# Four buffers for float32 queries and keys, fill products through the first tile, and POOL in place of ACT for one step of the weight conversion

## The chip, the cores and the metric

The kernel runs on one core of a Trainium2 chip. The metric is the device time of one execution in microseconds, as the median of several runs. Five engines work side by side, each through its own list of instructions in a fixed order: PE (matrix products), ACT and DVE (elementwise work), POOL, and SP, which here only starts transfers. "PEld" is the loading of the stationary operand of a product.

## The reference, cut to what matters

Attention over 4 batches of 8 heads, with 512 local and 32 global positions, is followed by two dense blocks on 2304 tokens of width 512:

```python
out = concat([softmax(q_g k_all^T) v_all, softmax(mask(q_l k_l^T), q_l k_g^T) v_all])   # window of +-32
h = x @ w_in                                  # 512 -> 2048
x = g(h) @ w_out                              # g: 0 below -1, h above 1, (h + 1)^2 / 4 between
y = ((x @ w_a) * (x @ w_b)) @ w_out2          # 512 -> 1536 -> 512
```

The weights arrive as float64.

## The kernel before, in words

The tokens go through in six tiles of up to three blocks of 128. One attention item is one block and one pair of heads; a tile has 12 items (the last one differs). `att_atoms` runs items as a pipeline: scores `s` of item k (L187, two products), softmax (L200 on DVE, L204 on ACT, L208 to L211), transposes `tp` of item k-2 (L217), their copy on ACT (L221), values `o` of item k-3 (L227), and a copy to `xraw` (L231). Items of the first nine blocks hold q and k in float32 (`qk`, loaded at L158 into a tag with 2 buffers, up to 3 items ahead, L342); later ones hold split halves (`qkd`, `qs`, `kh`, `kl`). The first four items are each followed by two products of the identity matrix with itself that nobody reads (`warm`, L192, `NWARM` and `WARM_ITEMS`).

Tile 0's attention runs first, alone, with a step of the weight stream at every eighth piece of it. Then `x_split` makes float32r halves of its result (L402 on ACT, L403 on DVE) and the first dense block begins: `h_unit` (12 products into `hp`, L435 to L437 in the helper `mm3`) and `x_unit` (12 products into `acc`). The stages are: 6 units of tile 0 beside tile 1's attention, 16 units of tile 1, the other 10 units of tile 0, then tiles 2 to 5, each beside the attention of a later tile, and last the second dense block. Tile 0 is written to memory and read back in between (L416, L422).

A weight slice comes as 512 KB of float64 (`wraw`, L90) and is rebuilt as float32 in `w_conv`: the high word is scaled on ACT into `wt` (L98), then DVE shifts it (L99) and puts in sign and low bits (L100, L101); `split` then makes halves on ACT (L108) and DVE (L109). There are 68 such conversions: 32 of the first block's weights, of which 4 fall in tile 0's attention and the others in the next two stages, 24 of w_a and w_b after that, and 12 of the last weights. `wraw` has 2 buffers, `wt` 3. In the second stage a conversion is put behind the rectifier work of the unit before (`paced`).

The order on each engine comes from a scheduler that fills in from the code's order and from what each instruction waits for, so a small edit shifts rows far away.

Of the kernel before, what the change touches and what calls it, by code (L numbers as in the profile page):

```python
# [10 lines left out]
F32 = mybir.dt.float32  # L11
# [3 lines left out]
AF = mybir.ActivationFunctionType  # L15
# [4 lines left out]
P = 128  # L20
# [7 lines left out]
KW = SG + P + 2 * WIN  # L28
KC = KW // 2
# [9 lines left out]
W_DOWN = 2.0 ** -111  # L39
# [5 lines left out]


NNAT = 9
NWARM, WARM_ITEMS = 2, 4
FA = 6
START_ATOMS = 8  # L50
LEAD1 = 4
# [8 lines left out]
def body(tc, qk, qkd, vw, kg, vg, w1i, w1o, w2a, w2b, w2o, mask, out):  # L60
    nc = tc.nc
# [4 lines left out]
    ps = es.enter_context(tc.tile_pool(name="ps", bufs=4, space=PSUM))  # L66
# [4 lines left out]
    ident = cp.tile([P, P], F32, name="ident")  # L71
# [6 lines left out]
    def f32(t):  # L78
        return t.bitcast(F32)
# [13 lines left out]
    def w_conv():  # L93
        key, raw = wq.pop(0)
        low, high = raw[:, :, 0], raw[:, :, 1]
        t = sp["p"].tile([P, 512], I32, name="wt", bufs=sp["wt"])
        tf = f32(t)
        nc.scalar.activation(tf, f32(high), AF.Copy, scale=W_DOWN)  # L98
        nc.vector.tensor_scalar(t, t, 3, 0x7FFFFFFF, ALU.logical_shift_left, ALU.bitwise_and)  # L99
        nc.vector.scalar_tensor_tensor(t, high, -0x80000000, t, ALU.bitwise_and, ALU.bitwise_or)  # L100
        nc.vector.scalar_tensor_tensor(t, low, 29, t, ALU.logical_shift_right, ALU.bitwise_or)  # L101
        return key, tf
# [8 lines left out]
    def w_split():  # L111
        key, tf = w_conv()
        w = slot()
        split(w[:, 0], w[:, 1], tf)
        wslots[key] = w
# [23 lines left out]
    def new_xraw(t):  # L139
        xraw_cur[t] = [mp.tile([P, 384], F32, name=f"xraw{c}", bufs=1) for c in range(NC)]  # L140

    gp = {}

    class Local:
        def __init__(self, t, j, blk, p):
# [6 lines left out]
        def load(self):  # L152
            if self.stk:
                self.raw = gp["k"].tile([P, 2, P + KW], F32, name="qkd", tag="qkd", bufs=2)
                nc.sync.dma_start(self.raw, qkd[self.blk - NNAT, self.p])
            else:
                self.qk = gp["k"].tile([P, P + KW], F32, name="qk", tag="qkd", bufs=2)
                nc.sync.dma_start(self.qk, qk[self.blk, self.p])  # L158

        def prep(self):  # L160
# [28 lines left out]
        def fill(self):  # L189
            w = ps.tile([P, 512], F32, name="warm", tag="acc")  # L190
            for _ in range(NWARM):
                nc.tensor.matmul(w[:, :P], ident, ident, start=True, stop=True)  # L192

        def s_post(self):
            m = 1 if self.i == 0 else (2 if self.i == SL // P - 1 else 0)
            self.e = ap.tile([P, 2, KW], F32, name="e", tag="e", bufs=EBUFS)
            mn = ap.tile([P, 2], F32, name="mn", tag="mn", bufs=EBUFS)
            self.sm = ap.tile([P, 2], F32, name="sm", tag="sm", bufs=EBUFS)
            for h in range(2):
                nc.vector.tensor_tensor_reduce(  # L200
                    self.e[:, h], self.s[h], masks[:, m], -SCALE, 3.0e38,
                    ALU.add, ALU.min, mn[:, h:h + 1])
            for h in range(2):
                nc.scalar.activation(self.e[:, h], self.e[:, h], AF.Exp, bias=mn[:, h:h + 1],  # L204
                                     scale=-1.0, accum_out=self.sm[:, h:h + 1])
# [17 lines left out]
        def v_pe(self):  # L223
            self.o = ps.tile([P, P], F32, name="o", tag=self.tag)
            for c in range(2):
                for h in range(2):
                    nc.tensor.matmul(self.o[64 * h:64 * h + 64], self.v[:, c, 64 * h:64 * h + 64],  # L227
                                     self.pt[:KC, 2 * c + h], start=c == 0, stop=c == 1)

        def v_post(self):  # L230
            nc.vector.tensor_copy(xraw_cur[self.t][self.p][:, self.j * P:(self.j + 1) * P], self.o)  # L231
# [92 lines left out]
    items = []  # L324
    ends = {}
# [11 lines left out]
    def att_atoms():  # L337
        n = len(items)
        nl = nv = npr = 0
        started = set()  # L340
        for k in range(n + 3):
            while nl < min(k + (2 if nl < n and isinstance(items[nl], Glob) else 3), n):  # L342
                items[nl].load()
                nl += 1
            while npr < min(k + 1, nl):
                items[npr].prep()
                npr += 1
            while nv < min(k, n):
                items[nv].load_v()
                nv += 1  # L350
            if k < n and items[k].t is not None:
                it = items[k]
                it.s_pe()
                if k < WARM_ITEMS:
                    it.fill()
                it.s_post()
            if 1 <= k <= n and items[k - 1].t is not None:
                items[k - 1].norm()
            while npr < min(k + 2, nl):
                items[npr].prep()  # L360
                npr += 1
            if k < n and items[k].t is not None:
                yield k, 0
            if 2 <= k <= n + 1 and items[k - 2].t is not None:
                it = items[k - 2]
                it.t_pe()
                it.t_post()
                yield k, 1
            if 3 <= k and items[k - 3].t is not None:
                it = items[k - 3]  # L370
                if isinstance(it, Local) and it.t not in started:
                    started.add(it.t)
                    new_xraw(it.t)
                it.v_pe()
                it.v_post()
                yield k - 3, 2

    att = att_atoms()
    done = {"n": 0}

# [80 lines left out]
    acc = {}  # L461
# [112 lines left out]
    def w2_conv():  # L574
        r = w_conv()
        rawn[0] += 1
        raw_to(rawn[0] + sp["raw"])
        return r
# [108 lines left out]
    k = 0  # L687
# [83 lines left out]
    for u in range(len(units)):  # L771
        for kind in (0, 1):
            if kind == 0:
# [17 lines left out]
                if u in conv_at:  # L791
                    i = conv_at.index(u)
                    (nm, f2), tf = paced(w_conv)
                    nc.sync.dma_start(wd[f2]["ab".index(nm)], tf)
                    if i + 2 < len(ab2):
                        w_load(*ab2[i + 2])
# [152 lines left out]
```

## Time and profile before

| | us |
|---|---|
| median of 3 runs | 948.53 (947.63 to 950.57) |
| the profiled execution, its own time | 954.25 |
| its span, first to last instruction | 952.5 |
| busy: PE / DVE / ACT / POOL | 932.2 / 717.1 / 530.1 / 0.7 |
| first product of the first dense block | 49.97 from the start |
| tile 0's products begin again after the read back | 184.55 |

Busy times count an engine as busy while one of its instructions is under way. Products overlap, so PE's busy share says little about how dense they are; the step from one group of products to the next says more. The granted clock of PE is given as a share of full speed: 1.00 is 2.4 GHz, 0.50 is 1.2 GHz.

### The profile page before, as it was taken

The numbers are of one execution on the slowest core, as the hardware profiler recorded it, in microseconds if no ns is written. First come the engines' busy times: TensorE is split into PE (matmuls) and PEld (weight loads), VectorE is DVE, ScalarE is ACT, GpSimd is POOL, SyncE is SP. The second block draws the span as 40 slices with busy tenths as digits, with TensorE's granted clock in tenths as the row PEclk, the third lists the DMA queues.
The fourth block names the chain that finished last, engine by engine and source line by source line (L and its number), as shares of the span: only waits on it lengthen the run. The fifth ranks groups of instructions, "written<-read, shape, count | busy, mean of one in ns | idle before, by whom it ended". The sixth has DMA issues, their size and how long they took to land.

```text
span 952.5 us, 16671 instructions
## 1 busy us (share of the span) xinstructions
PE 932.2 (98%) x5964; PEld 840.9 (88%) x5964; DVE 717.1 (75%) x1863; ACT 530.1 (56%) x1271; POOL 0.7 (0%) x7
## 2 busy tenths in 40 slices
PE   6999999999999999999999999999999999999997
PEld 4577888899999999987889999999999999999996
DVE  5688999789877877764449968888896666877663
ACT  6677766566666766644445555555654444654441
POOL 0000000000000000000000000000000000000000
PEclk9699999999999999999999999999999999999999
DMA  5465555666534453323455323321241111131101
GB/s 174 151 214 164 177 161 168 219 223 211 178 117 156 128 162 112 120 94 103 133 194 183 96 77 115 95 68 51 69 147 45 45 45 49 42 121 56 56 12 56
DMA packets 59299, 114.05 MB, mean 120 GB/s; under 512 B 7248, under 2 KB 28368, under 8 KB 59216
## 3 DMA queue, kind: packets, MB, share of 16 engines
q1 hardware_dynamic: 59072, 112.81, 37.8%
q8 instruction: 47, 0.77, 0.3%
q14 instruction: 36, 0.29, 0.1%
q10 hardware_dynamic: 144, 0.17, 0.1%
HBM read 95.40 MB, written 17.56 MB: 119 GB/s over the span
## 4 chain that ended last, share of the span: by engine, by line
PE 90%; DMA 4%; DVE 3%; ACT 1%; issue 1%; SPq 0%; ACTq 0%; DVEq 0%
PE hp L435 7%; PE acc L435 6%; PE acc L436 6%; PE hp L437 6%; PE hp L436 6%; PE acc L437 6%; PE pb L596 5%; PE pb L597 5%; PE pb L594 5%; PE py L661 5%; PE py L662 5%; PE py L660 5%; PE px L594 4%; PE px L597 4%; PE px L596 4%; PE o L227 4%
## 5 line engine op out<-in xcount | busy, mean ns | idle before, releaser
L435 PE MATMUL hp<-xh,w 128*128 128x384 f32 (+1 forms) x384 | 130.7, 341 | 3.4 <-ACT xh L402 1.7
L435 PE MATMUL acc<-g,w 128*128 128x384 f32 (+1 forms) x384 | 131.1, 341 | 0.0
L436 PE MATMUL acc<-g,w 128*128 128x384 f32 (+1 forms) x384 | 127.0, 331 | 0.0
L437 PE MATMUL acc<-g,w 128*128 128x384 f32 (+1 forms) x384 | 125.6, 329 | 0.0
L437 PE MATMUL hp<-xl,w 128*128 128x384 f32 (+1 forms) x384 | 125.2, 327 | 0.0
L436 PE MATMUL hp<-xh,w 128*128 128x384 f32 (+1 forms) x384 | 125.1, 326 | 0.0
L108 ACT ACTIVATE w<-wt 128x512 fp32r<-128x512 f32 (+1 forms) x116 | 65.2, 563 | 72.6 <-PE pb L597 44.9
L596 PE MATMUL pb<-w 128*128 128x384 f32 (+1 forms) x288 | 94.7, 329 | 0.0
L597 PE MATMUL pb<-w 128*128 128x384 f32 (+1 forms) x288 | 94.3, 327 | 0.0
L594 PE MATMUL pb<-w 128*128 128x384 f32 (+1 forms) x288 | 93.8, 326 | 0.0
L723 ACT ACTIVATE r<-hp,half 128x384 f32<-128x384 f32 (+1 forms) x96 | 53.4, 557 | 55.1 <-PE hp L437 54.3
L435 PEld LDWEIGHTS hp<-xh,w 128*128 128x128 f32 x384 | 72.4, 189 | 10.8 <-issue 3.1
L724 DVE SCALAR_TENSOR_TENSOR m<-hp,r 128x384 f32<-128x384 f32 (+1 forms) x96 | 51.0, 532 | 39.9 <-ACT r L723 39.5
L661 PE MATMUL py<-w,g 128*128 128x512 f32 x204 | 80.7, 396 | 0.0
L662 PE MATMUL py<-w,g 128*128 128x512 f32 x204 | 80.7, 396 | 0.0
L660 PE MATMUL py<-w,g 128*128 128x512 f32 x204 | 79.7, 390 | 0.0
L435 PEld LDWEIGHTS acc<-g,w 128*128 128x128 f32 x384 | 72.4, 189 | 6.9 <-issue 5.3
L109 DVE TENSOR_TENSOR w<-wsum,w 128x256 fp32r<-128x256 f32 (+1 forms) x108 | 54.6, 507 | 29.8 <-ACT w L108 29.8
L728 ACT ACTIVATE g<-m 128x384 fp32r<-128x384 f32 (+1 forms) x96 | 48.3, 503 | 47.9 <-DVE m L725 47.4
L436 PEld LDWEIGHTS acc<-g,w 128*128 128x128 f32 x384 | 72.5, 189 | 2.1 <-issue 1.4
L437 PEld LDWEIGHTS acc<-g,w 128*128 128x128 f32 x384 | 72.2, 188 | 1.2 <-issue 1.0
L109 DVE TENSOR_TENSOR w<-wt,w 128x512 fp32r<-128x512 f32 (+1 forms) x116 | 70.2, 605 | 3.5 <-ACT w L108 1.7
(113 smaller groups left out, 2119.6 us busy)
## 6 DMA issues: line engine op xcount, KB each, us to landing
wt<-wd SPq DMA_DIRECT2D x72, 256.0 KB, 2.7
qkd<-in_qkd_dram SPq DMA_DIRECT2D x28, 352.0 KB, 3.1
wraw<-in_w1i_dram SPq DMA_DIRECT2D x16, 512.0 KB, 3.6
wraw<-in_w1o_dram SPq DMA_DIRECT2D x16, 512.0 KB, 3.4
v<-in_vw_dram SPq DMA_DIRECT2D x64, 112.0 KB, 2.4
qk<-in_qk_dram SPq DMA_DIRECT2D x36, 176.0 KB, 2.7
wraw<-in_w2a_dram SPq DMA_DIRECT2D x12, 512.0 KB, 3.9
wraw<-in_w2b_dram SPq DMA_DIRECT2D x12, 512.0 KB, 4.2
```

The lines of the kernel that those rows point to most:

```text
L108: nc.scalar.activation(hi, src, AF.Copy)
L109: nc.vector.tensor_tensor(lo, src, f32(hi), ALU.subtract)
L435: nc.tensor.matmul(acc, whi, xhi, start=first, stop=False)
L436: nc.tensor.matmul(acc, wlo, xhi, start=False, stop=False)
L437: nc.tensor.matmul(acc, whi, xlo, start=False, stop=last)
L594: nc.tensor.matmul(out[:, :n], w[:, 0, r], hi[:, c, :n], start=start and c == 0, stop=False, skip_group_check=True)
L596: nc.tensor.matmul(out[:, :n], w[:, 1, r], hi[:, c, :n], start=False, stop=False, skip_group_check=True)
L597: nc.tensor.matmul(out[:, :n], w[:, 0, r], lo[:, c, :n], start=False, stop=k in (1, 5, 6) and c == 1, skip_group_check=True)
L660: nc.tensor.matmul(a, gh[:, c], w[:, 0], start=f == 0, stop=False)
L661: nc.tensor.matmul(a, gh[:, c], w[:, 1], start=False, stop=False)
L662: nc.tensor.matmul(a, gl[:, c], w[:, 0], start=False, stop=f == NF2 - 1)
L723: at["act"] = nc.scalar.activation(r[:, :W], hp[:, :W], AF.Relu, bias=half, scale=0.5 / W_UP).ins
```

## The change

There are three edits. First, float32 `qk` tiles rotate over four buffers: two of the old tag and one each in the tags of `kh` and `kl`, which the later items use; the load may now run up to five items ahead instead of three. Second, `warm` follows each of the 12 items of tile 0 instead of four, and a new `bridge` of 8 such products is placed behind the last value product of tile 0. Third, the scaling of the high word in `w_conv` is a `tensor_scalar_mul` on POOL instead of an ACT instruction, for all 68 conversions.

```diff
-NWARM, WARM_ITEMS = 2, 4
+NWARM, WARM_ITEMS = 2, 12
+NBRIDGE = 8
...
-        nc.scalar.activation(tf, f32(high), AF.Copy, scale=W_DOWN)
+        nc.gpsimd.tensor_scalar_mul(tf, f32(high), W_DOWN)
...
-                self.qk = gp["k"].tile([P, P + KW], F32, name="qk", tag="qkd", bufs=2)
+                n = nat["n"] % 4
+                nat["n"] += 1
+                if n < 2:
+                    self.qk = gp["k"].tile([P, P + KW], F32, name="qk", tag="qkd", bufs=2)
+                else:
+                    self.qk = gp["k"].tile([P, P + KW], F32, name="qk", tag=("kh", "kl")[n - 2], bufs=1)
...
+        def bridge(self):
+
+            with tc.issue_after(self.oi):
+                w = ps.tile([P, 512], F32, name="bridge", tag="acc")
+                for _ in range(NBRIDGE):
+                    nc.tensor.matmul(w[:, :P], ident, ident, start=True, stop=True)
...
-            while nl < min(k + (2 if nl < n and isinstance(items[nl], Glob) else 3), n):
+            while nl < n and nl < k + (2 if isinstance(items[nl], Glob) else 3 if items[nl].stk else 5):
...
+                if k - 3 == ends[0] - 1:
+                    it.bridge()
```

In the rows of the changed program the lines are those of its own file: scores are L194 (before L187), `warm` L199 (L192), transposes L231 (L217), values L241 (L227), `mm3` L452 to L454 (L435 to L437), the exponential L218 (L204), the copies L224 and L235 (L210 and L221), the scaling L99 (L98) and the shift L100 (L99).

SP's first transfers, before:

```order
1 L158 DMA qk<-in_qk_dram 128x352 x2
2 L90 DMA wraw<-in_w1i_dram 128x1024 x2
3 L158 DMA qk<-in_qk_dram 128x352 x2
4 L174 DMA v<-in_vw_dram 112x256 x3
5 L158 DMA qk<-in_qk_dram 128x352 x2
```

and SP's first transfers now:

```order
1 L165 DMA qk<-in_qk_dram 128x352 x4
2 L91 DMA wraw<-in_w1i_dram 128x1024
3 L165 DMA qk<-in_qk_dram 128x352
4 L91 DMA wraw<-in_w1i_dram 128x1024
5 L165 DMA qk<-in_qk_dram 128x352
```

The third and fourth `qk` stand ahead of both weight slices, and the second slice stands behind a fifth `qk` that reuses a buffer.

PE's first rows, before (`s` are scores, two rows to an item):

```order
7 L187 MATMUL s_208<-qk 128x224
8 L192 MATMUL warm<-ident 128x128 x6
9 L217 MATMUL tp<-ident,e 112x128 x4
10 L187 MATMUL s_209<-qk 128x224
11 L192 MATMUL warm<-ident 128x128 x2
12 L217 MATMUL tp<-ident,e 112x128 x4
13 L227 MATMUL o<-pt,v 64x128 x4
```

and the same place on PE now:

```order
9 L194 MATMUL s_251<-qk 128x224
10 L194 MATMUL s_252<-qk 128x224
11 L199 MATMUL warm<-ident 128x128 x6
12 L231 MATMUL tp<-ident,e 112x128 x4
13 L199 MATMUL warm<-ident 128x128 x2
14 L231 MATMUL tp<-ident,e 112x128 x4
15 L241 MATMUL o<-pt,v 64x128 x4
16 L199 MATMUL warm<-ident 128x128 x2
17 L231 MATMUL tp<-ident,e 112x128 x4
18 L241 MATMUL o<-pt,v 64x128 x4
```

Before, three and a half items' scores stood ahead of the first fill; now five items' scores do, and a fill of two goes on with every item.

PE where tile 0's attention ends, before (`hp` is the first dense product):

```order
53 L227 MATMUL o<-pt,v 64x128 x4
54 L187 MATMUL s_607<-qk 128x224
55 L187 MATMUL s_608<-qk 128x224
56 L217 MATMUL tp<-ident,e 112x128 x4
57 L227 MATMUL o<-pt,v 64x128 x4
58 L435 MATMUL hp<-xh_635,w 128x384
59 L436 MATMUL hp<-xh_635,w 128x384
```

and PE at that place now:

```order
63 L241 MATMUL o<-pt,v 64x128 x4
64 L231 MATMUL tp<-ident,e 112x128 x4
65 L452 MATMUL hp<-xh_672,w 128x384
66 L241 MATMUL o<-pt,v 64x128 x4
67 L206 MATMUL bridge<-ident 128x128 x8
68 L453 MATMUL hp<-xh_672,w 128x384
69 L454 MATMUL hp<-xl_677,w 128x384
```

The first dense product moved ahead of the last value product, and the bridge stands between it and the others.

ACT's first rows, before:

```order
3 L204 ACTIVATE e,sm<-e,mn 128x224 x4
4 L210 ACTIVATE e<-e,sm 128x224
5 L98 ACTIVATE wt<-wraw 128x512
6 L204 ACTIVATE e,sm<-e,mn 128x224 x2
7 L210 ACTIVATE e<-e,sm 128x224
8 L204 ACTIVATE e,sm<-e,mn 128x224
9 L98 ACTIVATE wt<-wraw 128x512
```

and ACT's first rows now:

```order
3 L218 ACTIVATE e,sm<-e,mn 128x224 x4
4 L224 ACTIVATE e<-e,sm 128x224
5 L218 ACTIVATE e,sm<-e,mn 128x224 x2
6 L224 ACTIVATE e<-e,sm 128x224
7 L218 ACTIVATE e,sm<-e,mn 128x224 x2
8 L235 ACTIVATE pt<-tp 112x512
9 L224 ACTIVATE e<-e,sm 128x224
```

The scaling rows left ACT; they are 68 rows on POOL now, and DVE's shift waits for POOL where it waited for ACT.

## Rows read from the trace of the kernel before

**Rows 1.** Busy time of each engine in stretches of the span, PE's granted clock.

```profile
core 0: us, PE busy (x) PEld busy (x) DVE busy (x) ACT busy (x) POOL busy (x), PEclk, DMA share, GB/s
...
15.00:25.00 10.00, 9.28 (x78) 5.91 (x78) 8.68 (x40) 9.06 (x27) 0.00 (x0) 1.00 0.64 210
28.90:45.60 16.70, 16.32 (x73) 9.78 (x72) 9.35 (x43) 10.38 (x33) 0.00 (x0) 0.50 0.50 151
50.00:185.00 135.00, 132.32 (x829) 112.08 (x830) 124.63 (x349) 95.58 (x230) 0.00 (x0) 1.00 0.56 178
185.00:900.00 715.00, 713.85 (x4641) 661.21 (x4641) 536.12 (x1322) 383.83 (x906) 0.00 (x0) 1.00 0.36 112
900.00:952.50 52.50, 47.48 (x273) 42.87 (x271) 27.19 (x59) 17.27 (x39) 0.00 (x0) 0.98 0.11 36
```

**Rows 2.** Chain that ended last, up to 50 us: start, duration, what.

```profile
5.07 3.69 DMA qk<-in_qk_dram
...
8.90 1.83 PE s L187 x6
10.73 2.86 PE warm L192 x12
13.59 0.85 PE tp L217 x4
...
15.36 0.64 PE warm L192 x4
...
22.18 4.86 DMA qk<-in_qk_dram
...
27.80 2.40 DMA qk<-in_qk_dram
```

**Rows 3.** Timeline of PE up to 50 us: start, duration, group, idle time ahead.

```profile
16.36 0.66 PE L227 MATMUL o<-pt,v 112*64 112x128 f32 x8
16.95 0.65 PE L187 MATMUL s<-qk 64*128 64x224 f32 x4
17.53 0.65 PE L217 MATMUL tp<-ident,e 128*112 128x128 f32 x4
18.11 0.66 PE L227 MATMUL o<-pt,v 112*64 112x128 f32 x8
...
24.78 0.66 PE L227 MATMUL o<-pt,v 112*64 112x128 f32 x8
27.08 0.65 PE L187 MATMUL s<-qk 64*128 64x224 f32 x4 [1.65 <-DMA qk<-in_qk_dram]
...
47.66 0.66 PE L227 MATMUL o<-pt,v 112*64 112x128 f32 x8
49.97 0.44 PE L435 MATMUL hp<-xh,w 128*128 128x384 f32 x1 [1.65 <-ACT xh L402]
```

**Rows 4.** Chain, later in the half-clock stretch: start, duration, what.

```profile
33.50 1.04 PE s L187 x2
34.54 1.03 PE tp L217 x4
35.57 1.05 PE o L227 x8
```

**Rows 5.** The step that moves, over the whole span: busy, mean ns, idle ahead of it.

```profile
L98 ACT ACTIVATE wt<-wraw 128x512 f32<-128x512 f32 x68 | 45.1, 665 | 17.0 <-DVE w L109 7.3 <-DMA wraw<-in_w1o_dram 3.7 <-DMA wraw<-in_w1i_dram 3.2
```

**Rows 6.** All groups of POOL above 128x1, and one of 128x1: busy, mean ns.

```profile
masks.py:199 POOL TENSOR_SCALAR_AFFINE_SELECT ident<-ident 128x128 f32<-128x128 f32 x1 | 0.3, 293 | 0.0
masks.py:197 POOL MEMSET ident<- 128x128 f32 x1 | 0.2, 204 | 0.3 <-POOLq L938 0.3
L74 POOL MEMSET half<- 128x1 f32 x1 | 0.1, 98 | 0.0
```

**Rows 7.** Groups of DVE between 50 and 185 us: busy, mean ns.

```profile
L100 DVE SCALAR_TENSOR_TENSOR wt<-wraw,wt 128x512 int32<-128x512 int32 x29 | 19.9, 687 | 0.1
L109 DVE TENSOR_TENSOR w<-wt,w 128x512 fp32r<-128x512 f32 x28 | 19.3, 689 | 2.1 <-ACT w L108 1.7
```

More of the change, by code (lines that the diff above doesn't have):

```diff
@@ L142, in body @@
     gp = {}
+    nat = {"n": 0}
     class Local:
@@ L226, in v_pe @@
                 for h in range(2):
-                    nc.tensor.matmul(self.o[64 * h:64 * h + 64], self.v[:, c, 64 * h:64 * h + 64],
-                                     self.pt[:KC, 2 * c + h], start=c == 0, stop=c == 1)
+                    self.oi = nc.tensor.matmul(
+                        self.o[64 * h:64 * h + 64], self.v[:, c, 64 * h:64 * h + 64],
+                        self.pt[:KC, 2 * c + h], start=c == 0, stop=c == 1).ins
         def v_post(self):
```

## The prediction

> **What bounds the kernel now.** I first read the busy times by stretch [rows 1]. From 185 to 900 us PE is busy 713.85 of 715 us at full clock, while DVE has 715 - 536 = 179 us to spare. There the products are the bound, so whatever moves the start of that stretch moves the end one for one. From 900 us the tail keeps its shape. What can change lies ahead of 185 us, in two parts.
>
> Tile 0's attention, to 49.97 us, is not bound by one engine. The chain of waits [rows 2] shows three causes. The first is loads of q and k: PE waits for them at 8.90 (issued at 5.07, when a buffer came free), at 27.08 (1.65 us idle [rows 3]) and around 28 to 30. The second is the clock: between 28.9 and 45.6 us it is granted at 0.50, that is 1.2 GHz, and each group of products steps by 1.04 us [rows 4] where it steps by 0.58 at full speed [rows 3]. It fell after PE had run dry waiting for a load, and rose after PE had run on without a break. The third is ACT, 9.06 of 10 us busy between 15 and 25 us [rows 1], while the clock was up.
>
> The stages from 50 to 185 us run both PE (132.3 of 135) and DVE (124.6 of 135) nearly full [rows 1]. DVE's spare time there is only 10 us, and 29 of the 68 conversions fall into it [rows 7].
>
> **The change part by part.** *Start of the pipeline.* Four `qk` now load at once, but in PE's new order the scores of the fifth item stand ahead of the first fill, and that item's load reuses a buffer, as the one did that was issued at 5.07 and took 3.69 us [rows 2]. So the fifth item's scores again start near 8.9. Before, six rows (1.83 us) followed there, now four (1.2 us); the fill of 2.86 us then begins near 10.1 instead of 10.73. The first transposes start near 13 instead of 13.59, and the first values (16.36 before [rows 3]), with one more fill ahead, near 15.4: 1 us gained.
>
> *Pace of the items.* From the first to the twelfth value group the trace needs 47.66 - 16.36 = 31.3 us, 2.85 us for each of 11 steps [rows 3]. At full clock four steps took 24.78 - 16.36 = 8.4 us, 2.10 each, of which PE's own work is 0.58 + 0.58 + 0.59 = 1.75 [rows 3]. A fill of two products adds 0.64 [rows 2], so PE needs 2.39 an item if it never stalls, and 2.10 + 0.64 = 2.74 if the fill adds to every stall. I take 2.5, nearer to the first: a fill runs mostly where PE would wait, and ACT, which held that stretch at 91%, loses 0.665 us with each of the four conversions [rows 1, 5]. This supposes that the clock stays up; PE then works 2.39 of 2.5 us, more densely than in any part of the stretch in which it was up before. The loads that broke the pace now have four buffers and are issued two items earlier. Eleven steps take 27.5 us instead of 31.3: 3.8 gained, with bounds of 26.3 (5.0 gained) and 30.1 (1.2 gained). The last two or three items have no fill, which gives up to 1.9 more at the lower end, and ACT and DVE have worked ahead by then; if PE never stalled at all, its groups from the first transposes on sum to 9 x 0.58 for scores, 9 x 0.64 for fills, 12 x 0.58 and 12 x 0.59 = 25 us, and the end would come 10 us earlier.
>
> *Bridge.* 8 products are 16 records, four fills of 0.64 = 2.6 us. Before, PE idled 1.65 us at that place for ACT's split [rows 3], which the bridge covers. Some dense products could have run there instead, so I charge 0.5 us (0 to 1). The first part thus gains 1 + 3.8 - 0.5 = 4.3; with the ACT relief beyond the pace and the missing last fills I take **5 us**, between 2 and 10.
>
> *Scaling on POOL, its own price.* The trace has no such instruction on POOL. The nearest rows are a MEMSET and an AFFINE_SELECT of 128x128 at 204 and 293 ns, against 98 ns for 128x1 [rows 6]. Per further element that is 0.83 to 1.5 ns, so 512 elements take an estimated 0.52 to 0.87 us; ACT took 0.665 [rows 5]. One conversion's chain changes by -0.14 to +0.21 us. I take no change: POOL has nothing else to do and can start when the slice lands, where ACT had to come round to it. ACT also no longer stands still for slices: it waited 3.7 + 3.2 us on such transfers with rectifier work queued behind it [rows 5]. PE's whole idle time from 50 to 185 us is 2.7 us [rows 1], so this is worth 0 to 2.7; I take **1 us**. The queue behind the wait is now DVE's, whose shift waits for POOL; behind it stand the rectifier steps and the softmax of the next item. It waited for ACT in the same way before, so nothing is added unless POOL is slow.
>
> *Scaling on POOL, its price for DVE.* While POOL reads and writes the buffers, DVE may be slowed. No row shows the two at work together, so I bound it: between nothing, and DVE standing still for the whole of each POOL instruction. 29 instructions of 0.52 to 0.87 us are 15 to 25 us, less the 10 us DVE has to spare: 5 to 15 us. I take **2 us**, nearer to nothing, because DVE also has steps with one operand in these buffers, and its spare 10 us absorb the first part. The 35 conversions behind 185 us lie beside 179 us of spare DVE time and 331 us of spare ACT time [rows 1] and cost nothing; if that cover failed, 35 x 0.87 = 30 us would be at stake.
>
> *SP.* In the new order the two first slices of w_a and w_b stand ahead of tile 0's read back instead of between its parts. PE's wait there is part of the 2.7 us above; I change nothing for it, with 1 us either way.
>
> **Sum.** -5 - 1 + 2 = -4 us. The profiled execution took 954.25 us (span 952.5) and would take 950.25. The median of the runs, 948.53, is 5.7 lower than the profiled execution; the same 4 us give **944.5 us**.
>
> **The rivals.** *POOL holds DVE up (slower).* Place: 50 to 185 us, where DVE is 92% busy. In the trace the two-operand steps fill much of DVE there, 19.9 and 19.3 us for two of its groups alone [rows 7], and POOL's instruction comes exactly where DVE works through the conversion before. The price is the 5 to 15 us above, plus some 2 us in tile 0's attention, against the 6 gained: -6 + 7 = +1 to -6 + 17 = +11, that is 949.5 to 959.5. It decides from about 0.6 us of delay to each of the 29. For it: DVE's small reserve. Against it: nothing in the trace, since POOL does nothing in these stretches [rows 1].
>
> The Trainium skill names this mechanism (GPSIMD Engine Reference, section Key points): the engine shares its SBUF interfaces with VectorE, and contention arises with two-input instructions and two-port modes. No run here shows it yet. By that rule the time would lie in this rival's range and not at the sum's.
>
> *The clock falls all the same.* The fills cost 0.64 us at full clock and twice that at 0.50. If PE again runs dry and the last five items go at half speed, each takes 3.1 [rows 4] + 1.28 = 4.4 us instead of 2.5, 9.5 us more than forecast: 944.5 + 9.5 = 954. For it: the waits for ACT and DVE stay. Against it: the long waits for loads, after which it fell, go.
>
> *The gain is swallowed.* The fills add to every stall (2.74 an item), ACT's relief finds no taker, and DVE loses 3 to 4 us: about 947 to 950, no change that counts.
>
> *The items run as PE can.* Pace 2.39 and no cost on DVE: -9 to -12, that is 937 to 940.
>
> **How the numbers follow.** About 0.3% (2.8 us) is what a measurement of this kernel can tell from no change, so faster means below 945.7 and slower above 951.4. Forecast, 940 to 947: 0.47, three quarters of it below 945.7. Items at PE's pace: 0.19, all faster. Swallowed: 0.12, no change. POOL holds DVE up: 0.17, two thirds of it slower. Clock falls: 0.05, slower. That gives faster 0.35 + 0.19 = 0.54, no change 0.12 + 0.12 + 0.06 = 0.30, slower 0.11 + 0.05 = 0.16. The range leaves out the ends: 936.5 to 953.
>
> **What would show it.** In the profile after: the first dense product near 44 to 45 us instead of 49.97; the clock at 1.00 from 15 us on; the value groups 2.4 to 2.7 us apart; POOL's 68 instructions at 0.5 to 0.9 us; DVE's L100 and L109 (one line lower or so) still at 0.69 us between 45 and 180 us; tile 0's products back at 180 us instead of 184.55. I am wrong if those DVE groups grow by 0.2 us or more, if POOL's instruction takes over 1 us, or if the clock drops again before the first dense product.

## The result, and the profile after

The changed kernel takes 958.11 us (median of 10 runs, 956.25 to 959.47), the kernel before 953.97 us beside it: a ratio of 1.0064, with an interval of 1.0041 to 1.0088 (the quotient of the two medians is 1.0043; the kernel before varies much, 947.63 to 959.22 us in ten executions). It is slower by about 6 us, where the forecast was 944.5 us with a range up to 953. Of the 13.6 us between the forecast and the measured time, 5.4 lie in the kernel before, whose median was 948.53 us where the forecast started and 953.97 here; the rest is a change of +4 us instead of -4. The profiled execution of the changed kernel took 959.04 us, its span is 957.3 us.

Busy time of each engine by stretch, as in [rows 1], now of the changed kernel:

```profile
core 0: us, PE busy (x) PEld busy (x) DVE busy (x) ACT busy (x) POOL busy (x), PEclk, DMA share, GB/s
15.00:25.00 10.00, 10.00 (x85) 7.10 (x85) 9.37 (x39) 8.65 (x27) 3.20 (x2) 1.00 0.59 186
28.90:45.60 16.70, 15.99 (x131) 11.91 (x130) 15.88 (x62) 14.87 (x44) 4.66 (x3) 1.00 0.84 266
50.00:185.00 135.00, 127.17 (x779) 107.72 (x778) 118.34 (x320) 75.68 (x185) 44.50 (x27) 0.99 0.50 159
185.00:900.00 715.00, 711.85 (x4604) 655.11 (x4604) 535.91 (x1312) 360.26 (x864) 55.06 (x34) 1.00 0.35 110
900.00:957.30 57.30, 52.26 (x302) 47.44 (x300) 31.48 (x70) 19.44 (x44) 0.00 (x0) 0.98 0.12 37
```

The start did better than forecast. The clock is at 1.00 where [rows 1] show 0.50, and PE has no idle time between 15 and 25 us. The timeline of PE shows the first and the twelfth value group, the bridge, the dense products behind it, and far below the first product on tile 0's x that was read back:

```profile
14.16 0.66 PE L241 MATMUL o<-pt,v 112*64 112x128 f32 x8
...
38.85 0.66 PE L241 MATMUL o<-pt,v 112*64 112x128 f32 x8
39.44 2.05 PE L206 MATMUL bridge<-ident 128*128 128x128 f32 x16
41.25 0.42 PE L453 MATMUL hp<-xh,w 128*128 128x384 f32 x1
...
182.10 0.41 PE L452 MATMUL hp<-xh,w 128*128 128x384 f32 x1 [0.93 <-DMA xh<-x0d]
```

In [rows 3] the first value group began at 16.36 us and the dense products at 49.97 us; they now begin 2.2 and 8.7 us earlier (one dense product stands alone still earlier, at 38.50). For the read back the kernel before needs a second look. The product at 184.55 us, named in its table, is the fourth one on the x read back, the first that PE is seen waiting for. The first one is this:

```profile
181.26 0.44 PE L435 MATMUL hp<-xh,w 128*128 128x384 f32 x1
```

The same product begins at 182.10 us in the changed kernel, 0.8 us later, so nothing is left there of the 8.7 us. From it to the end of the span the kernel before needs 952.5 - 181.26 = 771.2 us, this one 957.3 - 182.10 = 775.2. The order of the products around it differs from kernel to kernel, so kernels are compared below by a count: the 529th product of the first dense block (22 units of 24 products are behind it) begins at 187.7 us before and at 186.9 now, and the last of its 2304 at 560.0 and 561.2. Either way the loss lies on both sides of this point, 8 to 9.5 us ahead of it and 4 to 5.6 behind.

Between 50 and 185 us PE gets through 779 instructions instead of 829, and DVE through 320 instead of 349, though it is less busy (118.34 us, before 124.63). What DVE waited for stands in the groups of the conversion, over the span (busy us, mean ns of one, idle time ahead of it and what ended it); the first answers to [rows 5], the next to [rows 7], and the last two are the step behind the scaling, now and before:

```profile
L99 POOL TENSOR_SCALAR wt<-wraw 128x512 f32<-128x512 f32 x68 | 111.2, 1636 | 552.1 <-DVE w L110 134.8 <-DMA x1r<-x1d 131.7 <-DMA wraw<-in_w2a_dram 73.8
...
L101 DVE SCALAR_TENSOR_TENSOR wt<-wraw,wt 128x512 int32<-128x512 int32 x68 | 47.1, 694 | 0.6
...
L100 DVE TENSOR_SCALAR wt<-wt 128x512 int32<-128x512 int32 x68 | 29.2, 429 | 33.7 <-POOL wt L99 33.7
```

```profile
L99 DVE TENSOR_SCALAR wt<-wt 128x512 int32<-128x512 int32 x68 | 28.7, 423 | 11.3 <-ACT wt L98 11.0
```

POOL's step takes 1.64 us on average, 1.51 at the least, where ACT's took 0.665. The step behind it is DVE's shift, the first that needs POOL's result: DVE stood still for 33.7 us ahead of it, where it was 11.3 us before. DVE's step with two operands hardly grew: 694 ns over the span, against 687 between 50 and 185 us in [rows 7].

### The profile page after: what moved, and what is told of

The parts are those of the page before. It is cut to its first block, busy times and chain, and to the rows that moved or that the text cites. A ratio compares the mean times of both kernels' runs of the same rounds, so it can differ in the third digit from the quotient of the medians.

```text
span 957.3 us, 16872 instructions
## 1 busy us (share of the span) xinstructions
PE 935.9 (98%) x6012; PEld 843.8 (88%) x6012; DVE 727.1 (76%) x1863; ACT 493.4 (52%) x1203; POOL 111.9 (12%) x75
## 4 chain that ended last, share of the span: by engine, by line
PE 72%; issue 12%; DVE 7%; DMA 4%; POOL 3%; ACT 1%; POOLq 0%; ACTq 0%; DVEq 0%; SPq 0%
PE hp L452 6%; PE hp L454 5%; PE acc L452 5%; PE hp L453 5%; PE acc L453 5%; PE acc L454 5%; PE py L678 4%; PE py L679 4%; PE pb L613 4%; PE pb L614 4%; PE pb L611 4%; PE py L677 4%; PE o L241 3%; POOL wt L99 3%; PE px L611 3%
## 5 line engine op out<-in xcount | busy, mean ns | idle before, releaser
L99 POOL TENSOR_SCALAR wt<-wraw 128x512 f32<-128x512 f32 x68 | 111.2, 1636 | 552.1 <-DVE w L110 134.8
L452 PE MATMUL hp<-xh,w 128*128 128x384 f32 (+1 forms) x384 | 131.3, 342 | 6.3 <-DVE mn L214 2.3
L452 PE MATMUL acc<-g,w 128*128 128x384 f32 (+1 forms) x384 | 131.2, 342 | 0.0
L454 PE MATMUL hp<-xl,w 128*128 128x384 f32 (+1 forms) x384 | 126.4, 330 | 1.1 <-DVE xl L420 1.0
L454 PE MATMUL acc<-g,w 128*128 128x384 f32 (+1 forms) x384 | 126.6, 330 | 0.5 <-DVE g L746 0.5
L452 PEld LDWEIGHTS hp<-xh,w 128*128 128x128 f32 x384 | 72.6, 189 | 14.2 <-issue 4.5
L452 PEld LDWEIGHTS acc<-g,w 128*128 128x128 f32 x384 | 72.4, 189 | 6.7 <-issue 5.7
L454 PEld LDWEIGHTS hp<-xl,w 128*128 128x128 f32 x384 | 72.6, 189 | 2.3 <-DVE xl L420 2.0
L454 PEld LDWEIGHTS acc<-g,w 128*128 128x128 f32 x384 | 72.4, 188 | 2.1 <-issue 1.2
```

What stands on the lines that cost most here:

```text
L99: nc.gpsimd.tensor_scalar_mul(tf, f32(high), W_DOWN)
L452: nc.tensor.matmul(acc, whi, xhi, start=first, stop=False)
L454: nc.tensor.matmul(acc, whi, xlo, start=False, stop=last)
```

## Experiments

Ratios are against the kernel before, executed beside each run; its medians were 951.89 to 953.97 us (954.28 beside one run); where they are turned into microseconds, it is with 952.5. "The mark" is the first product on tile 0's x read back that PE waits for; the rows below end there. It isn't the same product in every kernel, so where times of two kernels are compared, it is with the same count of products, or by the start of the 529th. As every edit moves the order of other rows, a difference of a few us between two kernels can hold some of that too. The names used in the expectations: theory A says that DVE stands in its own order behind a scaling step that takes too long; E that the loop through two raw tiles grew; D that POOL's accesses slow DVE. F to H are about the start.

### What the parts are worth

The change without POOL, and POOL without the rest of the change:

```
buffers, fills, bridge:  after.py, line 99
-        nc.gpsimd.tensor_scalar_mul(tf, f32(high), W_DOWN)
+        nc.scalar.activation(tf, f32(high), AF.Copy, scale=W_DOWN)
POOL alone:  before.py, line 98, the same edit the other way
```

> The changed kernel with the scaling put back on ACT, so that only the buffers, the fill products and the bridge are left of the change. Theory A (the scaling by POOL is the whole loss, because DVE waits in its own order for a step of 1.5 us): the start's gain of about 8.7 us, read from the first dense products (49.97 us before, 41.25 us after), stays to the end, so 7 to 9 us less than before, a ratio of 0.990 to 0.993. Rival B (the gain at the start is lost later whatever does the scaling, since another limit sets the dense part): within 3 us of before, 0.997 to 1.003. Rival C (more fill products cost clock later): as the changed kernel, 1.004 to 1.009.

> The kernel before with the scaling by POOL as its only change. Theory A: the loss of about 14 to 15 us that the changed kernel hides behind its shorter start stands alone, a ratio of 1.013 to 1.017, with some 6 us of it up to tile 0's read-back products and 6 to 7 us behind 185 us. Rival B: nothing to about 6 us, 1.000 to 1.006, the rest being of the start's own making.

Without POOL: 947.94 us, ratio 0.9953 (0.9931 to 0.9975), 4.5 us faster. POOL alone: 965.66 us, 1.0145 (1.0112 to 1.0178), 14 us slower, as theory A had it. POOL's scaling is the loss. (With POOL alone the dense products begin at 44.98 us, 5.0 earlier than before, and the 529th at 193.0, 5.3 later.) But the rest brought half of the 9 us expected of it, so neither A nor B holds whole: the changed kernel's early dense products were in part POOL's work. Two runs put POOL on either side of the sixth conversion, which is about where tile 0's attention ends; the second of them has > in place of <=:

```
+        nconv["n"] += 1
+        if nconv["n"] <= 6:
             nc.gpsimd.tensor_scalar_mul(tf, f32(high), W_DOWN)
+        else:
+            nc.scalar.activation(tf, f32(high), AF.Copy, scale=W_DOWN)
```

> The changed kernel with POOL scaling only the first six conversions, those that lie in tile 0's attention, and ACT all the others. Both theories A and E: the start keeps POOL's gain (first run of dense products at 41 us, where the run with ACT's scaling had 42.8 and the changed kernel 41.25), and nothing is lost later, so 1 to 2 us below the run with ACT's scaling: 0.991 to 0.996 of before. Rival: the dense part's pace is set elsewhere and takes the 1.5 us back, 0.995 to 0.998.

> The changed kernel with ACT scaling the first six conversions and POOL all the later ones. If POOL's gain in the first six (6 to 7 us between the two runs that differ in them alone) and its loss behind them add, 5 to 7 us above the changed kernel: 1.011 to 1.015 of before, with POOL's loss in the dense part then 15 to 18 us. If the early gain is only lead that the dense part gives back when POOL scales there, as the changed kernel: 1.004 to 1.008.

POOL in the first six conversions only: 942.38 us, 0.9886 (0.9851 to 0.9920). POOL in all but these: 964.59 us, 1.0123 (1.0090 to 1.0157). The two divisions agree with each other. POOL in the first six gains 6.4 us (0.9886 against 0.9953) or 5.6 (1.0064 against 1.0123); POOL in the rest costs 17.0 us (1.0064 against 0.9886) or 16.2 (1.0123 against 0.9953). The early gain was expected at 1 to 2 us. The 529th product agrees: it begins at 181.7 us with ACT everywhere and at 176.7 with POOL early, at 192.0 with POOL late and at 186.9 in the changed kernel, so 5 us gained early and 10 lost behind, in both pairs. Its place is the stretch behind the attention: from 40 to 100 us PE does 412 instructions with POOL in the first six and 387 with ACT, because there DVE has finished the fourth weight at 37.5 us (with ACT at 41.0) and the sixth at 48.4 (with ACT at 53.4). ACT, busy 12.86 of 15 us between 15 and 30 us without POOL, came round to the slices late; POOL takes them as they land.

### What POOL costs behind the start

> The scaling back on ACT, as in the run with buffers, fill products and bridge alone, and in addition POOL scales the same high words once more, in four steps of 128x128 into a spare tile that nobody reads: added work, which changes no result. POOL then reads and writes the on-chip memory as much as in the changed kernel, but DVE waits for none of it. Theory A (the wait in DVE's order): within 2 us of the run without POOL's work, 0.990 to 0.994 of before. Rival D (POOL's accesses slow DVE's steps): as slow as the changed kernel, 1.004 to 1.009, with DVE's two-input steps of 128x512 well over 0.70 us in the rows.

```
+        nc.scalar.activation(tf, f32(high), AF.Copy, scale=W_DOWN)
+        spare = cp.tile([P, P], F32, name="spare", bufs=1)
+        for i in range(4):
+            nc.gpsimd.tensor_scalar_mul(spare, f32(high[:, i * P:(i + 1) * P]), W_DOWN)
```

951.15 us, 0.9981 (0.9957 to 1.0005): 2.7 us over the run without POOL's work, and 8 us under the changed kernel. Up to the mark DVE has the same work in both, and these rows (stretch, its length, busy us and instructions of PE, PEld, DVE, ACT, POOL, then clock and DMA) show what POOL does to it; first without POOL's added work, then with it:

```profile
0.00:177.88 177.88, 169.42 (x1100) 138.67 (x1100) 154.12 (x484) 130.34 (x330) 0.73 (x7) 1.00 0.59 185
```

```profile
0.00:180.02 180.02, 170.25 (x1099) 138.74 (x1100) 159.75 (x483) 130.42 (x330) 89.12 (x138) 1.00 0.58 183
```

DVE's 483 instructions take 5.6 us more while POOL works 88 us beside them, and the mark comes 2.1 us later. The intervals of the two runs overlap, so D is at most a small part: POOL worked longer here than in the changed kernel (89.12 us to the mark, there 55.64). The result is over the 0.990 to 0.994 of theory A, whose control was over its own range too. The Trainium skill (GPSIMD Engine Reference, section Key points) says that this engine shares SBUF interfaces with VectorE and contends with instructions that have two inputs. The trace agrees in direction: of the two two-operand steps on the raw words one went from 687 to 708 ns, the other from 685 to 687.

Next, DVE's wait itself. The changed kernel and the one with POOL in the first six conversions differ only behind the sixth, and up to their marks PE has done the same 1091 instructions. The same row for the one and for the other:

```profile
0.00:182.10 182.10, 168.86 (x1091) 138.62 (x1092) 156.84 (x475) 112.22 (x291) 55.64 (x41) 0.99 0.56 179
```

```profile
0.00:171.87 171.87, 164.31 (x1091) 137.15 (x1092) 154.70 (x482) 125.78 (x322) 10.08 (x13) 1.00 0.60 189
```

And DVE's waits for the scaling in these stretches, from the list of waits (us in total, times, longest), in the same order:

```profile
DVE wt L100 <- POOL wt L99: 15.0, 11, 2.5
```

```profile
DVE wt L106 <- POOL wt L103: 1.8, 1, 1.8
DVE wt L106 <- ACT wt L105: 0.9, 2, 0.7
```

The marks lie 10.2 us apart. DVE waits 15.0 - 2.7 = 12.3 us longer for the scaling, and its steps take 156.84 - 154.70 = 2.1 us longer; together that is more than the 10.2, so some of it is covered. PE's clock has a share too: it fell for some 3 us after PE had stood still for DVE, which is worth about 1.7 us (last section). The pair with ACT in the first six shows the same: with POOL behind them DVE waits 12.0 us up to the mark for its scaling, with ACT 2.5, and the 529th products lie 10.3 us apart. ACT, relieved, is 13.6 us less busy in the changed kernel, and no gain of it shows.

If POOL only has to start sooner, writing its step at the load should do:

```
     def w_load(key, src):
         ...
+        t = sp["p"].tile([P, 512], I32, name="wt", bufs=sp["wt"])
+        nc.gpsimd.tensor_scalar_mul(f32(t), f32(raw[:, :, 1]), W_DOWN)
         wq.append((key, raw, t))
```

> The changed kernel with POOL's scaling written at the load of the words, not at their conversion, with a third word tile in the second staging pool (two in the changed kernel), for 56 of the 68 conversions; the last 12 are scaled by ACT. POOL is then done long before DVE comes to the tile. Theory A: DVE no longer waits for POOL and ACT has 0.67 us less to do at each conversion, so as fast as the run with ACT's scaling or up to 4 us faster: 0.987 to 0.993 of before. Rival D (POOL's accesses slow DVE): 1.002 to 1.008.

954.74 us, 1.0024 (1.0002 to 1.0045): a miss, 7 us above the run with ACT, and 13 above the one with POOL in the first six only, whose early gain this kernel has too. It lies in D's range, but the wait in DVE's order stayed: 11.6 us for POOL up to the mark. The timeline between 110 and 118 us shows why POOL is not early (start, duration, engine and line, in brackets the idle time ahead):

```profile
110.93 0.98 DVE L110 SCALAR_TENSOR_TENSOR wt<-wraw,wt 128x512 int32<-128x512 int32 x1
...
111.98 0.33 SPq L91 DMA_DIRECT2D wraw<-in_w1i_dram  x1
...
115.54 1.77 POOL L94 TENSOR_SCALAR wt<-wraw 128x512 f32<-128x512 f32 x1 [3.30 <-DMA wraw<-in_w1i_dram]
...
117.34 0.43 DVE L108 TENSOR_SCALAR wt<-wt 128x512 int32<-128x512 int32 x1 [1.42 <-POOL wt L94]
```

DVE's last read frees a raw tile at 111.91, the load is issued at once and lands at 115.5, POOL starts in the same moment and takes 1.77 us, and DVE, which has come to that conversion, waits 1.42 us. So it is on the whole: over the 7th to the 32nd conversion POOL starts 0.16 us after the words land, here and in the changed kernel. There is no earlier moment for POOL, and the run doesn't test what a finished step ahead of DVE would be worth. This suggested theory E and a third raw tile, in two pairs that differ in who makes room for it:

```
-    sp["raw"], sp["wt"] = 2, 3
+    sp["raw"], sp["wt"] = 3, 3
-                    sp["raw"], sp["wt"] = 2, 2
+                    sp["raw"], sp["wt"] = 3, 2
-EBUFS = 4
+EBUFS = 3
...
-                    [P, 512], F32, name="x1", tag="y", bufs=2)
+                    [P, 512], F32, name="x1", tag="y", bufs=1)
```

That is the first pair. The second has 3, 2 in the first edit, so two scaled tiles in place of three, and leaves the score tiles at four; both have one output tile `y` instead of two.

> The changed kernel, with POOL's scaling at every conversion, and a third tile for the raw words in the two staging pools that have two. The room comes from one output tile instead of two and three attention score tiles instead of four. Theory E (the loop of two raw tiles: a tile is refilled in 3.5 us after DVE's last read, then POOL takes 1.55 us, then DVE reads it; POOL's extra 0.9 us lengthens that loop, and PE waits for it): with a third tile the loop is no limit, so within 3 us of the same kernel with ACT's scaling, 0.985 to 0.997 of before. Theory A (DVE in order behind POOL's step, whatever the loads do): still 6 us or more over the same kernel with ACT's scaling, 1.000 to 1.008.

> The same third raw tile and the same smaller tiles with the scaling back on ACT: the control for the run with POOL. Theory E: two tiles were already enough with ACT's 0.67 us, so within 3 us of the run with buffers, fill products and bridge alone, 0.992 to 0.999 of before; a gain of 5 us or more over that run would say that the loop of two raw tiles bounds the kernel with ACT too.

First pair: 955.87 us with POOL, 1.0042 (1.0020 to 1.0063), and 956.77 with ACT, 1.0043 (1.0023 to 1.0062). They are equal, as E expected of them, but the control is 9 us slower than with two raw tiles and four score tiles, so the smaller tiles cost more than the difference that was looked for, and the pair also mixes in POOL's early gain. The second pair keeps the score tiles, and its control has POOL in the first six:

> The changed kernel with three raw tiles instead of two in both staging pools, two scaled tiles instead of three in the first of them, and one output tile instead of two to make the room; the attention score tiles stay four. POOL scales everywhere. Theory E (the loop of two raw tiles carries the loss up to 400 us): within 6 us of its control, in which ACT scales all but the first six, with what is left lying behind 400 us, 0.990 to 0.997 of before. Theory A (DVE's order carries it): 12 us or more over the control, 1.002 to 1.010.

> The control: the same three raw, two scaled and one output tile, with POOL scaling only the first six conversions and ACT the others. With ACT's 0.67 us two raw tiles were enough, so theories A and E both expect it where the run with two raw tiles and POOL in the first six lies, 0.986 to 0.992 of before.

POOL everywhere: 958.36 us, 1.0060 (1.0039 to 1.0082). The control: 947.37 us, 0.9939 (0.9917 to 0.9962), which is itself 5 us over the run with two raw tiles and misses its range, so the smaller tiles cost here too. Between the two lie 11.5 us, where two raw tiles showed 17. So E falls as the main cause, and keeps a part: with POOL everywhere, PE does 1407 instructions between 185 and 400 us with three raw tiles and 1389 with two, and up to the mark DVE's waits for POOL are 6.0 us (15.0 in the changed kernel); the 529th product lies 5.9 us behind the control's (184.1 and 178.2), where with two raw tiles it was 10.2. A's 12 us were nearer.

The last test lengthens the same chain without POOL: behind the first six conversions ACT scales twice over.

```
         if nconv["n"] <= 6:
             nc.gpsimd.tensor_scalar_mul(tf, f32(high), W_DOWN)
         else:
             nc.scalar.activation(tf, f32(high), AF.Copy, scale=W_DOWN)
+            nc.scalar.activation(tf, f32(high), AF.Copy, scale=W_DOWN)
```

> The changed kernel with POOL scaling the first six conversions and ACT every later one twice over, the same step written two times, which changes no result: the chain from the landed words to DVE grows by 0.67 us as it does by 0.9 us with POOL, and POOL does nothing. Theories A and E (the length of the step): 0.67/0.9 of POOL's 17 us, some 10 to 13 us over the run in which ACT scales once, 0.999 to 1.003 of before. Rival D (POOL's accesses or POOL's hand-over are the cost): within 3 us of that run, 0.986 to 0.992.

944.22 us, 0.9915 (0.9887 to 0.9944), not told apart from the run with one step (0.9886, 0.9851 to 0.9920), and far from the 10 us that A and E expected. It lies in D's range, but what D names isn't the cause either: POOL's accesses came to 3 us at most above, and POOL's hand-over is quick, as in the timeline above POOL ends at 117.31 us and DVE starts at 117.34. DVE's waits up to the mark, with ACT twice:

```profile
DVE wt L107 <- ACT wt L106: 1.2, 2, 1.1
```

ACT's two steps are 1.33 us, POOL's one is 1.54 to 1.64; DVE waits 1.2 us for the one and 15.0 us, in the changed kernel, for the other. And the chain with ACT twice is not the shorter one: from the landing of the words to the end of the scaling, the 7th to the 32nd conversion take 2.12 us in the median with it, 1.70 in the changed kernel and 0.76 with ACT once. So it isn't the length alone. What differs is the order of DVE's steps, which is fixed when the kernel is built: counted in that order for 28 conversions behind the start, DVE's first step of a conversion stands within two steps of the last read of the conversion before it, which frees a raw tile, in 10 cases with POOL late, in 9 in the changed kernel, in 7 with ACT behind the first six (8 with ACT everywhere), and in 3 with ACT twice. With a doubled ACT step other work was put in between; with POOL's it was not. That this order makes the difference is argued from the count, not shown: no run changed the order alone, so it stays open how the 12 to 15 us divide between POOL's length and an order that doesn't fit it.

### Why POOL's step takes 1.54 us

The high words lie 8 bytes apart, and that was a suspect. A run like the one with the spare tile had POOL read the finished, dense words instead:

```
-            nc.gpsimd.tensor_scalar_mul(spare, f32(high[:, i * P:(i + 1) * P]), W_DOWN)
+            nc.gpsimd.tensor_scalar_mul(spare, tf[:, i * P:(i + 1) * P], W_DOWN)
```

> As the run in which POOL scales the high words once more into a spare tile (added work that nobody reads, four steps of 128x128 for each conversion, ACT doing the real scaling), but POOL reads the finished, dense words of the scaled tile instead of the high words 8 bytes apart. If the spacing makes POOL slow: 0.35 to 0.45 us a step, where the spaced one took 0.665. If POOL's rate on float32 is what it is: 0.60 to 0.70 us.

First the spaced, then the dense input:

```profile
L102 POOL TENSOR_SCALAR spare<-wraw 128x128 f32<-128x128 f32 x272 | 180.9, 665 | 447.5 <-DMA wraw<-in_w2o_dram 217.8 <-DMA wraw<-in_w2a_dram 69.7 <-DMA wraw<-in_w2b_dram 69.3
```

```profile
L105 POOL TENSOR_SCALAR spare<-wt 128x128 f32<-128x128 f32 x272 | 179.0, 658 | 480.0 <-DVE wt L103 405.7 <-DVE sm L226 34.0 <-DVE sm L225 22.7
```

665 and 658 ns: the spacing costs nothing that shows. (950.24 us in its one run, beside 954.28.) The step is slow by itself: 128 columns take 665 ns and 512 take 1636, about 2.5 ns for each further column. An AFFINE_SELECT of the same 128x128 took 293 ns [rows 6].

### What the start is worth, and what it didn't need

All with ACT's scaling, except where POOL early is named: there POOL scales the first six. Against the changed kernel the first three have these values:

```
buffers:          NWARM, WARM_ITEMS = 2, 4;  no bridge
buffers, bridge:  NWARM, WARM_ITEMS = 2, 4
fills, bridge:    n = nat["n"] % 2;  qk loaded three items ahead, not five
```

> Of the change only the four buffers of float32 q and k and the deeper prefetch: ACT scales, four items carry fill products as before, no bridge. Theory F (the fill products hold the clock at 1.00 from 15 us on and the buffers only let the items follow one another): the clock falls again between the fill products and the dense part, so less than half of the start's gain, a ratio of 0.997 to 1.001 and a first dense product at 46 to 50 us. Rival (the buffers are the gain, since the loads were the wait): 0.994 to 0.997 and a first dense product at 43 to 45 us.

> Of the change only the fill products at twelve items and the bridge: two buffers of q and k, loaded three items ahead as before, ACT scales. The clock stays at 1.00 up to the dense part, where the kernel before has 0.60 from 30 to 50 us, but the loads still wait for buffers. Theory G (the clock's fall costs the start its time): first dense product at 42 to 45 us, 0.994 to 0.998 of before. Theory H (the loads set the start, and fill products cost PE time): 47 us or later, 0.998 to 1.003.

> Four buffers, fill products at four items as before, and the bridge of sixteen products, scaling by ACT: it splits the 4 us by which fill products and bridge together made the run with the buffers alone slower. If the fill products cost it (PE is busy 15.00 of 15 us between 15 and 30 us with them), within 2 us of the buffers alone: 0.989 to 0.993 of before. If the bridge costs it, because the dense part waits behind it: 0.994 to 0.997.

> Four buffers of q and k and the deeper prefetch, fill products at four items as in the kernel before, no bridge, and POOL scaling only the first six conversions. If POOL's scaling gains in the attention stage because ACT is full there (4.00 of 4 us in several stretches of the run with the buffers alone), this lies 3 to 7 us below that run: 0.983 to 0.988 of before. If the gain of the run with POOL in the first six conversions came from the fill products' full PE, nothing: 0.990 to 0.993.

> Four buffers, fill products at four items as in the kernel before, the bridge, and POOL scaling only the first six conversions. If the parts add (buffers and bridge 0.9894, POOL's first six 3.7 us less without the many fill products): 0.983 to 0.987 of before. If POOL's first six and the bridge bring the same microseconds: 0.986 to 0.990.

| kernel | us | ratio (interval) |
|---|---|---|
| buffers, fills, bridge | 947.94 | 0.9953 (0.9931 to 0.9975) |
| fills, bridge | 945.92 | 0.9936 (0.9912 to 0.9960) |
| buffers | 944.07 | 0.9909 (0.9880 to 0.9939) |
| buffers, bridge | 942.85 | 0.9894 (0.9864 to 0.9924) |
| buffers, fills, bridge, POOL early | 942.38 | 0.9886 (0.9851 to 0.9920) |
| buffers, bridge, POOL early | 941.86 | 0.9878 (0.9844 to 0.9912) |
| buffers, POOL early | 940.19 | 0.9870 (0.9838 to 0.9903) |

Theory F fell: the buffers alone keep the clock. They also did better than the rival had it: the first dense product begins at 36.8 us. From 30 to 50 us, where the kernel before fell to 0.50, both the run with the buffers alone (first two rows) and the one with fills and bridge alone (third) have 1.00:

```profile
15.00:30.00 15.00, 13.83 (x102) 8.49 (x102) 14.08 (x59) 14.37 (x45) 0.00 (x0) 1.00 0.73 211
30.00:50.00 20.00, 18.83 (x127) 13.46 (x126) 17.99 (x65) 16.75 (x46) 0.00 (x0) 1.00 0.76 244
```

```profile
30.00:50.00 20.00, 18.29 (x149) 13.43 (x148) 17.99 (x72) 17.29 (x49) 0.00 (x0) 1.00 0.77 237
```

So G is right that the clock's fall cost the start its time, and either remedy takes it away: 8.7 us for the buffers, 6.1 for fills and bridge. The executions of the kernel before say the same: seven with a mean granted clock of 0.999 or 1.00 took 946.4 to 948.9 us, five with 0.983 to 0.985 took 957.3 to 959.6. So where the clock hardly fell, that kernel took about what buffers, fills and bridge take together (947.94), and most of what those three bring is the clock. Together they bring 4.5 us, by these medians less than each alone; only against the buffers are the intervals nearly apart. With both, PE is the bound, as this row of the run with all three shows:

```profile
15.00:30.00 15.00, 15.00 (x122) 10.35 (x118) 11.94 (x50) 12.86 (x39) 0.00 (x0) 1.00 0.60 177
```

PE is busy 15.00 of 15 us, while DVE drops from 14.08 to 11.94. A value group comes every 2.05 us with the buffers alone and every 2.31 with the fills on top of them. The bridge costs nothing that shows (0.9894 beside 0.9909). POOL in the first six gives the run with the buffers alone another 3.7 us, with intervals that overlap; the three fastest kernels aren't told apart by their intervals, and all beat both kernels of this case by over 1%.

## Why the prediction was wrong, point by point

- **Start, pace and bridge: -5, bounds 2 to 10.** Right in its sum, in part by luck: without POOL the change gains 4.5 us (2.4 to 6.6), but that run lacks the relief of ACT on which the 5 counted, and its dense products begin 7.2 us earlier (at 42.79). The parts were off. The pace of 2.5 us an item became (38.85 - 14.16) / 11 = 2.24 in the changed kernel, near PE's own work there: in a step around 25 us the timeline has 0.58 for scores, 0.55 for a fill, 0.53 for transposes and 0.59 for values. The fill had been put at 0.64, and the bridge at 2.6 where 1.8 (39.44 to 41.25) was measured. The clock held as forecast. What the forecast didn't weigh is that the buffers alone bring 8.7 us, so that eight more fills had little stall left to fill and cost PE time.
- **ACT's relief: -1, bounds 0 to 2.7.** Mis-sized, and looked for in the wrong stretch. It was taken from PE's idle time between 50 and 185 us. In the first six conversions POOL gains 5.6 to 6.4 us, since weights are ready 3.5 to 5 us sooner when the dense part begins; behind them no gain of ACT's relief shows.
- **POOL's price by itself: 0.52 to 0.87 us, "I take no change".** This is the first of the two steps that failed. The estimate went from MEMSET and AFFINE_SELECT [rows 6] to a TENSOR_SCALAR, and rows of one operation didn't carry to another: 1.54 us in the median, nearly twice the upper bound. The text named it, "POOL's instruction takes over 1 us", as a sign of being wrong. The Trainium skill (GPSIMD Engine Reference, section 3.1) gives 769 ns for 512 elements in its best loop; the measured step is twice that, and the measurement decides.
- **"Nothing is added unless POOL is slow."** The condition came true, in DVE's order: 15.0 us of waits up to the mark. That slowness by itself makes the waits is not shown, as ACT's doubled step was hardly waited for.
- **POOL's price for DVE: +2, bounds 0 and 15.** As contention alone it was about right: 2 to 6 us of stretched steps up to the mark, partly covered. The same range had the size of the whole loss up to the mark (10.2 us against the run with POOL early), but for another reason, the wait.
- **"The 35 conversions behind 185 us cost nothing."** This is the second step that failed. From the mark, the same product in both, to the end the changed kernel needs 775.2 us, the run with POOL early 940.9 - 171.87 = 769.0: 6.2 us. Spare DVE time over 715 us was an average; a wait at the head of DVE's order isn't covered by spare time elsewhere, and with three raw tiles part of it went.
- **Sum.** -4.5 for the start, -6 for POOL early, +17 for POOL late is +6.5, and +6 was measured. Two rivals came true at once: the items ran at PE's pace, and POOL held DVE up. The measured change, +4 to +6, lies in the range of the second, +1 to +11, which got 0.17; but that range was priced for the stretch up to 185 us alone, where 10 of POOL's 16 to 17 us fell, and by POOL's accesses, which were the smaller part; the larger was DVE's wait. The forecast gave that rival too little, since a price for an operation that no row showed was bounded by rows of other operations.

## What to carry to other kernels

An operation that the trace doesn't have on that engine has no price yet: rows of other operations there bound it badly, and the chance of a bad price belongs into the range. Here a step was worth moving to an idle engine where its old engine was full and its reader came late, and cost time where its reader was nearly full and in order; split such a move by place, and look at the reader's waits and not at its average spare time. Two remedies for one stall need not add, so try each alone, as the second can cost what it no longer saves.

## What the runs showed of the hardware

- POOL's TENSOR_SCALAR on float32, 128x512, takes 1.51 us at the least and 1.64 on average, ACT's ACTIVATE of the same tile 0.665. Reading words 8 bytes apart made no difference (665 against 658 ns for 128x128).
- POOL working beside DVE stretched DVE's steps little: 5.6 us on 154 us of DVE's work with 88 us of POOL's beside it.
- In the changed kernel the clock dropped once in the dense part: 0.83 on average between 120 and 130 us, where the run with ACT has 1.00. It stood at 0.50 from about 122 to 126 us, and the lack over the ten us is worth 10 x (1 - 0.83) = 1.7 us. The runs with POOL alone and with POOL late show such a fall in the dense part too, around 150 us (with POOL alone also around 245), and those with ACT there none. PE had been idle for 2.35 us just ahead, on DVE, as its timeline shows:

```profile
121.71 0.44 PE L452 MATMUL hp<-xh,w 128*128 128x384 f32 x1 [2.35 <-DVE mn L214]
```
